# Attention with beacon keys, then an MLP: q and k turned by VectorE in 32x32 squares and placed through DRAM, one ring of four PSUM banks, seven MLP slots a step

One core of one Trainium2 chip. The metric is the device time of one execution in microseconds (us), median of several runs. The trace of a run shows one profiled execution, whose span is about 1.7 us shorter than its own time.

## The reference, cut to what matters

```python
B, H, S, Nb, D = (8, 8, 576, 16, 64)            # q, k, v: [B, H, S, D] f32; beacon_k, beacon_v: [B, H, Nb, D]
k_all = np.concatenate([beacon_k, k], axis=2)   # beacons are seen by every query, the rest is causal
scores = scale * np.matmul(q, k_all.transpose(0, 1, 3, 2))
scores = np.where(causal, -1000000000.0, scores)
a = softmax(scores)                             # written out in the reference
attn = np.matmul(a, v_all)
x = attn.transpose(0, 2, 1, 3).reshape(B * S, H * D)   # 4608 x 512
h = x @ w_in                                    # 512 -> 2048
g = h * (1.0 / (1.0 + np.exp(-1.702 * h)))
return g @ w_out                                # 2048 -> 512
```

The inputs of the attention are normal numbers times 0.1, so the scores are near zero and the softmax weights nearly equal. That matters for reading the experiments: **the comparison with the reference hardly sees q and k**.

## The kernel before

One step is one pair of heads of one batch: scores, exponentials, masks, and the product with v (AV) of the step before. Between these parts the loop deals out "slots" of the MLP, four matmuls of 512 columns each. The parts that the change touches:

```python
    psu = ctx.enter_context(tc.tile_pool(name="psu", bufs=3, space=bass.MemoryType.PSUM))
    pso = ctx.enter_context(tc.tile_pool(name="pso", bufs=1, space=bass.MemoryType.PSUM))
# ... (cut)
    def load_qk(b, h0, h1):
            # batches 1 to 7: one token a partition, 64 numbers (128 bytes in f16) a piece
            for i in range(NSB):
                rows = min(P, S - i * P)
                nc.gpsimd.dma_start(
                    out=t[0:rows, i, h0:h1, :],
                    in_=src[b, h0:h1, i * P : i * P + rows, :].rearrange("h s d -> s h d"),
                )
# ... (cut)
    def tr_pair(b, p, which):          # q (which 0) or k (which 1) of a pair of heads
            u = psu.tile([P, S], F16, tag="u", name="u")
            for i in range(NSB):       # five transposes on TensorE
                rows = min(P, S - i * P)
                nc.tensor.transpose(
                    u[:, i * P : i * P + rows],
                    src[0:rows, i, 2 * p : 2 * p + 2, :].rearrange("r h d -> r (h d)"),
                    ident[0:rows, 0:rows],
                )
        # then a copy to qT on ScalarE or to kT on VectorE
# ... (cut)
    def norm(b, hf):                   # four products by the reciprocals, all on GpSimd
# ... (cut)
    def mlp2(g, mt, qt):               # a second-layer tile in four slots, in the one bank of pso
        if qt == 0:
            ops[0] = pso.tile([P, DMODEL], F32, tag="o", name="o")
# ... (cut)
    QUOTA = 8                          # slots a step, spread evenly between the parts of a step
```

The normalising of a half batch is a chain of its own: the softmax sums are gathered to `zc`, VectorE takes the reciprocals `rc`, these go to DRAM (`zd`) and are read back spread over the partitions (`rz`), and four products write xT, from which the first layer reads.

The softmax here doesn't subtract the row's maximum and nothing guards it: scores larger than these inputs give would overflow.

## Time and profile before

| | before |
|---|---|
| median time | 477.54 us (476.39 to 480.32, 4 runs) |
| span of the profiled execution | 474.5 us |
| busy: TensorE, VectorE, ScalarE, GpSimd | 396, 193, 223, 251 us |
| mean granted TensorE clock | 0.941 |
| first MLP slot | 89.8 us |

I keep the division of the span that the prediction uses: the time to the first MLP slot, the TensorE work counted from there (341 us with transposes, 321 without), the end after the last matmul (about 4 us), and what is left, called **idle** below. For the kernel before it is 474.5 - 89.8 - 341 - 4 = 40 us.

### The profile page before, as it was taken

To read this page: it belongs to the slowest core of one execution; us is meant where nothing else is said; L and a number is where in the kernel's file an instruction comes from. 1 tells how busy PE (TensorE), PEld (TensorE's weight loads), DVE (VectorE), ACT (ScalarE), POOL (GpSimd) and SP (SyncE) were. 2 spreads that over 40 slices of the span, in tenths; PEclk is the share of its full clock that TensorE was granted. 3 is DMA by queue.
4 is the path that set the end of the run, shared out by engine and by line. 5 is a ranking of instruction groups with operands and counts; after the bars stand their busy time and mean duration, and the time that the engine had idled before them with its cause. 6 is when DMAs were issued, how large, how long until landed. Compare 5 with 4: busy or idle time off the path is not lost.

```text
span 474.5 us, 6853 instructions
## 1 busy us (share of the span) xinstructions
PE 396.0 (83%) x2584; PEld 201.8 (43%) x2584; DVE 193.0 (41%) x410; ACT 222.8 (47%) x341; POOL 251.3 (53%) x348
## 2 busy tenths in 40 slices
PE   2505555889999999899989998999899999899985
PEld 1303333444444444444444456645444444444432
DVE  5403373755125522561256226622561373184410
ACT  3303433665456545664466446644665442263421
POOL 9945078489528952895379627954616250400000
PEclk9955675899999999999999999999999999999999
DMA  9999939959614981399129911990203112100111
GB/s 86 157 176 179 82 46 148 79 44 111 111 59 56 111 122 46 65 107 129 47 55 110 134 48 52 108 140 34 63 2 95 56 42 64 77 1 22 46 44 66
DMA packets 122016, 38.22 MB, mean 81 GB/s; under 512 B 109696, under 2 KB 115328, under 8 KB 121984
## 3 DMA queue, kind: packets, MB, share of 16 engines
q0 software_dynamic: 111424, 18.62, 54.9%
q1 hardware_dynamic: 10560, 19.18, 14.2%
q8 instruction: 20, 0.33, 0.3%
q14 instruction: 12, 0.10, 0.1%
HBM read 46.66 MB, written 9.58 MB: 119 GB/s over the span
## 4 chain that ended last, share of the span: by engine, by line
PE 59%; ACT 17%; POOL 7%; DMA 7%; DVE 5%; issue 4%; ACTq 0%; POOLq 0%; DVEq 0%
PE o L408 26%; PE u L382 19%; ACT E L252 8%; PE u L310 6%; ACT sig L391 5%; PE u L189 4%; DVE g L392 4%; PE s L244 3%; ACT osb L417 3%; DMA w<-in_moe_w_in_dram 3%; DMA bk<-in_beacon_k_dram 2%; POOL kn L114 1%; POOL vb L136 1%; DMA zc<-O 1%; POOL xT L354 1%
## 5 line engine op out<-in xcount | busy, mean ns | idle before, releaser
L382 PE MATMUL u<-xT,w 128*128 128x512 f16 (+1 forms) x640 | 144.7, 358 | 12.5 <-DVE g L392 12.4
L408 PE MATMUL o<-w,g 128*128 128x512 f16 x576 | 144.1, 379 | 9.7 <-ACT osb L417 9.7
L392 DVE SCALAR_TENSOR_TENSOR g<-sig,u 128x512 f16<-128x512 f16 x144 | 99.0, 687 | 104.9 <-ACT sig L391 104.8
L354 POOL TENSOR_TENSOR xT<-O,rz 64x576 f16<-64x576 f32 x64 | 89.6, 1400 | 79.9 <-DMA rz<-zd 76.3
L391 ACT ACTIVATE sig<-u 128x512 f16<-128x512 f32 x144 | 87.6, 609 | 77.3 <-PE u L382 72.9
L252 ACT ACTIVATE E<-s 128x1024 f16<-128x1024 f32 (+3 forms) x128 | 104.7, 876 | 14.8 <-PE s L244 8.8
L317 DVE COPY O<-u 128x288 f32<-128x288 f32 x128 | 56.3, 453 | 71.2 <-PE u L310 69.9
L382 PEld LDWEIGHTS <-w 128*128 128x128 f16 x640 | 56.8, 97 | 63.3 <-issue 20.4
L274 POOL TENSOR_SCALAR_AFFINE_SELECT E<-E 128x256 f16<-128x256 f16 (+2 forms) x120 | 43.1, 395 | 67.0 <-ACT E L252 66.3
L408 PEld LDWEIGHTS <-g 128*128 128x128 f16 x576 | 50.2, 97 | 63.1 <-issue 15.6
L310 PE MATMUL u<-E,vb 128*128 128x288 f16 (+6 forms) x576 | 69.5, 260 | 5.3 <-DVE O L317 5.1
L310 PEld LDWEIGHTS <-vb 128*128 128x128 f16 (+1 forms) x576 | 52.5, 104 | 36.8 <-issue 12.2
L417 ACT ACTIVATE osb<-o 128x512 f32<-128x512 f32 x36 | 21.5, 597 | 82.1 <-PE o L408 82.1
L244 PE MATMUL s<-qT,kT 64*128 64x80 f16 (+5 forms) x384 | 44.1, 307 | 18.4 <-ACT E L252 9.9
L196 ACT COPY qT<-u 128x576 f16<-128x576 f16 x32 | 20.5, 640 | 73.4 <-PE u L189 66.7
L244 PEld LDWEIGHTS <-kT 64*128 64x128 f16 x384 | 17.1, 99 | 58.6 <-issue 46.2
L114 POOL DMA_DIRECT2D kn<-in_k_dram x35 | 29.6, 883 | 5.9 <-DMA w<-in_moe_w_in_dram 5.9
L136 POOL DMA_DIRECT2D vb<-in_v_dram x36 | 29.7, 860 | 2.7 <-DMA w<-in_moe_w_out_dram 2.7
L198 DVE COPY kT<-u 128x576 f16<-128x576 f16 x32 | 15.7, 492 | 37.2 <-PE u L189 35.6
L114 POOL DMA_DIRECT2D qn<-in_q_dram x35 | 29.9, 884 | 0.0
L168 PE MATMUL u<-ident,bk 16*128 16x16 f16 x32 | 2.1, 170 | 28.2 <-DMA bk<-in_beacon_k_dram 28.2
L267 DVE TENSOR_TENSOR E<-E,keep 128x128 f16<-128x128 f16 (+2 forms) x80 | 17.1, 271 | 14.0 <-ACT E L252 13.6
(29 smaller groups left out, 108.8 us busy)
## 6 DMA issues: line engine op xcount, KB each, us to landing
rz<-zd SPq DMA_DIRECT2D x32, 288.0 KB, 4.4
out_dram<-osb SPq DMA_DIRECT2D x36, 256.0 KB, 2.0
qn<-in_q_dram POOLq DMA_DIRECT2D x28, 128.0 KB, 4.2
kn<-in_k_dram POOLq DMA_DIRECT2D x28, 128.0 KB, 4.4
vb<-in_v_dram POOLq DMA_DIRECT2D x21, 128.0 KB, 6.0
w<-in_moe_w_in_dram POOLq DMA_DIRECT2D x4, 512.0 KB, 9.3
w<-in_moe_w_out_dram POOLq DMA_DIRECT2D x4, 512.0 KB, 9.5
vb<-in_v_dram POOLq DMA_DIRECT2D x7, 112.0 KB, 3.3
```

What stands on the lines that cost most here:

```text
L114: nc.gpsimd.dma_start(out=t[0:rows, i, h0:h1, :], in_=src[b, h0:h1, i * P : i * P + rows, :].rearrange("h s d -> s h d"),)
L244: nc.tensor.matmul(sc[:, x, o : o + e - a], kT[r : r + 64, p, j * P : (j + 1) * P], qT[r : r + 64, p, a:e], start=True, stop=True,)
L252: nc.scalar.activation(out=E[:, :, choff[ci] : choff[ci] + o], in_=sc[:, :, 0:o], func=AFT.Exp, scale=0.125,)
L274: nc.gpsimd.affine_select(out=blk, in_=blk, compare_op=ALU.is_ge, fill=0.0, base=mc, pattern=[[0, 2], [1, w]], channel_multiplier=-1,)
L310: nc.tensor.matmul(u[:, lo - qa : hi - qa], lhs, E[0:kw, x, col : col + hi - lo], start=(n == 0), stop=(n == len(mm) - 1),)
L317: nc.vector.tensor_copy(out=O[:, p % 2, qa:qe], in_=u[:, :])
L354: nc.gpsimd.tensor_tensor(out=xT[r : r + 64, p, c : c + S], in0=O[r : r + 64, a, :], in1=rz[r : r + 64, a, :], op=ALU.mult,)
L382: nc.tensor.matmul(u[:, o : o + w], w1t[:, kp, nt * P : (nt + 1) * P], xT[:, kp, m : m + w], start=(kp == 0), stop=(kp == NKP - 1),)
L391: nc.scalar.activation(out=sig[:, :], in_=u[:, :], func=AFT.Tanh, scale=0.851)
L392: nc.vector.scalar_tensor_tensor(out=gts[g][:, nt, :], in0=sig[:, :], scalar=1.0, in1=u[:, :], op0=ALU.add, op1=ALU.mult,)
L408: nc.tensor.matmul(o[:, :], gts[g][:, nt, mt * P : (mt + 1) * P], w2t[:, nt, :], start=(nt == 0), stop=(nt == NNT - 1),)
L417: nc.scalar.mul(out=osb[:, :], in_=o[:, :], mul=0.5)
```

## The change

Its intent is to take the transposes off TensorE, which bounds the steady stage, and to give TensorE enough PSUM banks. q and k are loaded so that a partition holds 18 consecutive tokens of a head (pieces of 4.6 KB of the input). VectorE turns them in squares of 32x32. The turned squares don't lie on the partitions where the scores want them, so they are stored to DRAM and read back in place. The products are split between VectorE and GpSimd, all matmuls but the scores share one ring of four banks, and a step gets seven slots in lumps. The diff, cut to its core (the order of loads at the start, forty warm-up matmuls and the loop's rewriting are cut):

```diff
-    psu = ctx.enter_context(tc.tile_pool(name="psu", bufs=3, space=bass.MemoryType.PSUM))
-    pso = ctx.enter_context(tc.tile_pool(name="pso", bufs=1, space=bass.MemoryType.PSUM))
+    psu = ctx.enter_context(tc.tile_pool(name="psu", bufs=4, space=bass.MemoryType.PSUM))
# ...
+    def load_qk(b, g, which):
+        nc.gpsimd.dma_start(
+            out=nat[b][which][:, g, :, :].rearrange("p t d -> p (t d)"),
+            in_=(q, k)[which][b, g * HG : (g + 1) * HG].rearrange("h (r t) d -> (h r) (t d)", t=TPP),
+        )
# ...
-    def tr_pair(b, p, which):
# ...
+    def tr_group(b, g, which):
# ...
+        dst = t[:, :, off : off + S].rearrange("p e (r t) -> p t e r", t=TPP)
+        n = TPP // 2
+        for c in range(2):
+            nc.vector.transpose(
+                dst[:, c * n : (c + 1) * n, :, :],
+                src[:, g, c * n : (c + 1) * n, :],
+            )
+        d = dr.tile([2, P, w], F16, tag=f"d{which}", name=f"d{which}")
+        for e in range(2):
+            nc.sync.dma_start(
+                out=d.rearrange("l (y e r) s -> e (l y) r s", y=2, e=2)[e],
+                in_=t[:, e, lo : lo + w],
+            )
+        full = (qTs, kTs)[which][b % 2]
+
+        def place():
+            nc.sync.dma_start(
+                out=full[:, 2 * g : 2 * g + 2, 0:w],
+                in_=d.rearrange("l p s -> p l s"),
+            )
# ...
+        (nc.vector, nc.gpsimd)[y].tensor_tensor(      # the products, in norm()
# ...
+    def mlp2(g, mt):
+        o = psu.tile([P, DMODEL], F32, tag="u", name="u")
+        for nt in range(NNT):
# ... in the loop, a step:
+        norm(b3, p3 // 2, 1); norm(b3, p3 // 2, 3)    # two lines in the source
+        mlp(4)
+        norm(b3, p3 // 2, 0); norm(b3, p3 // 2, 2)    # two lines in the source
# ... av, reciprocals
+        mlp(1)
# ... scores
+        while places:
+            places.pop(0)()
# ... av with mlp(1) between its halves
+            places += [tr_group(b + 1, p - 1, 1), tr_group(b + 1, p - 1, 0)]
+        mlp(1)
```

## The prediction

Its sum came to 414 us in the span, 65 + 321 + 24 + 4, and was taken down to 410 for the time. What rested on figures that no trace of this case shows is cut from the text, terms of the sum among them: how a turn of 576 elements came to 0.755 us and the small one to its price (both are in the 3.2 us of a half batch and in VectorE's 252), how long the new stores and their reading back take, and so the two steps between the transposes at 11 us and the scores near 18. For the turns the trace of before gives nearly the same: L392's 0.687 us for 512 elements, taken in proportion, is 0.77 for 576 and 3.2 for a half batch (an estimate). For the trip to DRAM it gives nothing, so that its "hidden" and the 7 us of it before the first scores had no measured ground. That the new stores run on four engines was expected too; the trace of the kernel after shows it, see `e4_stores16`.

> **What bounds the kernel now.** I read the slice view first, then busy time by windows, then the order of instructions in time, the waits and the groups by form.
>
> ```profile
> PE   2505555889999999899989998999899999899985
> DVE  5403373755125522561256226622561373184410
> POOL 9945078489528952895379627954616250400000
> PEclk9955675899999999999999999999999999999999
> DMA  9999939959614981399129911990203112100111
> ```
>
> A slice is 474.5 / 40 = 11.9 us. TensorE (PE) is half idle for eight slices, some 94 us, and nearly full afterwards; in the first five slices the DMA engines are full instead. So there are two stages with different limits. The windows give the sizes (columns: window, its length, busy time and count of PE, weight loads, DVE, ACT, POOL, then granted clock, DMA share, GB/s):
>
> ```profile
> 0.00:94.00 94.00, 46.02 (x397) 27.84 (x398) 39.50 (x123) 34.35 (x47) 60.30 (x82) 0.71 1.29 117
> ...
> 190.60:238.80 48.20, 44.54 (x292) 21.91 (x292) 19.92 (x39) 25.95 (x41) 32.23 (x47) 1.00 0.80 85
> ...
> 412.00:474.50 62.50, 55.68 (x256) 24.72 (x253) 22.02 (x32) 24.35 (x41) 0.00 (x0) 0.99 0.10 38
> ```
>
> The middle line is one steady batch (four steps, 32 MLP slots): PE 44.5 of 48.2 us busy at full clock, every other engine under 33. The last line is the tail, MLP alone. In both, TensorE is the bound. The start is a chain of loads and waits. These are the two places where TensorE stands first for data, then for buffers:
>
> ```profile
> PE u L168 <- DMA bk<-in_beacon_k_dram: 28.2, 3, 18.8
> ...
> PE u L382 <- DVE g L392: 12.4, 20, 0.7
> ...
> PE o L408 <- ACT osb L417: 9.7, 25, 0.7
> ```
>
> The beacon load is queued behind the weights and the second batch's q and k, so it stands for all of them. The other two are bank waits: first-layer matmuls (L382) for a bank of the ring of 3, second-layer ones (L408) for their only bank.
>
> What TensorE spends on each kind of work I take from starts in the order of time, since the durations overlap their successors:
>
> ```profile
> 195.50 0.52 PE L189 MATMUL u<-ident,qn 128*128 128x128 f16 x5
> 195.95 1.04 PE L382 MATMUL u<-xT,w 128*128 128x512 f16 x4
> ...
> 205.74 0.38 PE L310 MATMUL u<-E,vb 128*128 128x288 f16 x3
> 206.11 1.02 PE L382 MATMUL u<-xT,w 128*128 128x512 f16 x4
> 207.14 0.66 PE L310 MATMUL u<-E,vb 128*128 128x224 f16 x6
> 207.64 1.93 PE L382 MATMUL u<-xT,w 128*128 128x512 f16 x8
> ```
>
> Five transposes cost 195.95 - 195.50 = 0.45 us; the two AV halves of a head 0.37 and 0.50, so one step (two heads) 1.74. Read the same way at 198.25 to 201.38, the scores of one step cost about 1.04.
>
> ```profile
> 403.87 3.61 PE L408 MATMUL o<-w,g 128*128 128x512 f16 x16 [0.69 <-ACT osb L417]
> 408.17 3.61 PE L408 MATMUL o<-w,g 128*128 128x512 f16 x16 [0.69 <-ACT osb L417]
> 411.62 14.84 PE L382 MATMUL u<-xT,w 128*128 128x512 f16 x68
> ```
>
> Sixty-eight dense matmuls take 411.62 to 426.30, so 0.216 us each and 0.864 a slot of four. Two L408 tiles in a row lose 0.69 each to the single bank.
>
> [...] No run yet shows a transpose, [...]the 512-element DVE operation L392 takes 0.687 us[...]. [...](the 9 KB store of the reciprocals lands in 1.9 us, the 256 KB output in 2.0). [...] The new stores have a slowest dimension of 4 on the DRAM side[...]; no transfer of before shows such a case.
>
> **The change part by part.** *TensorE loses its transposes.* In the stage that it bounds (from the first MLP slot at 89.8 us) these are 42 groups of five (two of batch 2, 40 of batches 3 to 7): 42 x 0.45 = 19 us, and 1 us for the beacon. All of it lies on the path.
>
> *VectorE gains them.* Per half batch: four transposes of 576[...] and a small one[...] = 3.2 us, 16 times: 52 us. It gains 32 of the 64 normalising products (576 elements, 0.755: 24 us) and loses the kT copies (15.7 + 1.5). 193 + 52 + 24 - 17 = about 252 us, far from a bound overall. ACT loses 32 copies of 0.64 = 20.5 us. POOL loses 32 products of 1.40 (45 us) and swaps 78 q/k load issues, 65 us with L107, for 32. Beside TensorE, all this is off the path.
>
> *The DRAM trip.* A half batch is stored at the end of one step and read back in the middle of the next. [...] In steady state the data is wanted two steps after the store or later: hidden. For batch 0 it is on the path.
>
> *The start.* q and k of batch 0 are 1.18 MB in f16; the weights moved at 176 GB/s of f16 (third and fourth slice), so 1.7 us each for the four loads, with v in f32 beside them. First k and q on chip at about 7 and 9 us, transposes to 11[...]: **scores start near 18 us against 9.0 before**. In exchange the weights and batch 1 are queued together and q/k no longer come in rows of 128 bytes: from the gate at 18.5 us, w1 12 us, q/k of batch 1 7 us, so its first half can be turned by 36. VectorE waits there in order, after step 1. Then steps 2, 3, 4 and 5 at about 5 us (masks 2.7, O copies 1.8, turning 3.2 in some) bring 58; batch 2's q and k, issued behind a product that waits for its reciprocals, add about 5. **First MLP slot: about 65 us**, against 89.8. It also comes half a step earlier in the schedule (after step 6's scores, not step 7).
>
> *The ring of 4.* Second-layer tiles no longer have a single bank: most of the 9.7 us wait goes, and perhaps half of the 12.4.
>
> *Seven slots a step* move work from steps to the tail. TensorE's sum stays.
>
> **The sum.** From the first slot, TensorE still has 288 slots x 0.864 = 248.7; scores of 25 steps 26; AV of 26.5 steps 46: 321 us. Before, the same count plus 20 of transposes is 341, and from 89.8 to the last matmul's end at 470.5 there are 381, so 40 us of idle and small losses between groups. I take 9 off for the L408 bank, 6 for the ring, 3 for waits that the transposes themselves had, and add 2 for VectorE blocked by 3.2 us of turning: 24. The end after the last matmul stays 4 us. 65 + 321 + 24 + 4 = 414 in the span. The time lies 3 us above the span (477.5 against 474.5), but I trust the idle term least and think it too high, since the change was plainly scheduled to keep TensorE fed: I choose **410 us**, a ratio of 0.86.
>
> **The rivals.** (1) *VectorE becomes the bound.* A step with 7 first-layer slots has 7 x 0.69 + 4 x 0.45 + 3.2 + 1.5 = 11.3 us on VectorE against 9.0 on TensorE. For it: the trace already shows TensorE waiting for L392. Against: once the second layer runs, a step has about three such slots, so 8.6 at most and 6 in the mean. If a transpose costs twice my 0.755, some 14 of the 16 turns would each cost 1 to 3 us: 425 to 435. (2) *The start is not shortened.* The DRAM trip, the gate and VectorE's in-order waits add up to a first slot at 85 or later: then only the 20 of transposes and 18 of waits come off, about 435. For it: DMA is full in the first five slices and its bytes stay. Against: the 128-byte rows go. (3) *The transfers collide*: 19 MB more traffic delay the reciprocals (4.4 us to landing), on which the products, now on VectorE too, wait in order. Against: the rest of the DMA work shrinks. It would cost 0.5 us in each of 25 steps: 420. (4) *Everything fits as planned*: first slot at 58, idle 12: 395.
>
> **Range and chances.** The start is uncertain by 7 us, idle by 9; together about 11, so 8 in 10 between 395 and 426. Even rivals 1 and 2 stay over 8% faster. Chances: faster 0.97, same 0.02, slower 0.01.
>
> **What would show it.** Right: transposes of 0.7 to 0.8 us, VectorE near 250 us; no TensorE wait for the output copy; steps of 9 to 9.7 us, a steady batch near 38; first slot between 58 and 72 us, a dense tail of about 100 us. Wrong: TensorE waiting long for L383 (the former L392) or for qT and kT in steady steps; transposes over 1.2 us; a first slot after 80 us; a granted clock below 0.95 after it.

## More of the kernel before

Idle is a remainder and holds more than standing still: where matmuls take longer than the dense time that the 341 are worked out from, the excess is in it too. Here TensorE's busy time from the first slot on is 353.9 us, so 13 of the 40 us are of that kind.

## The result, and the profile after

**542.45 us** (540.69 to 545.91, 4 runs), against 477.54 of before: ratio **1.136** [1.128, 1.143]. The prediction was 410, and faster. Ratios here are the mean time of one kernel's fast runs over that of the other's fast runs of the same rounds, so they are not quite the ratio of the quoted medians.

In the slice view of the kernel after, a slice is 541.5 / 40 = 13.5 us:

```profile
PE   7041223435986789669865958596669999999997
DVE  5970891599749965995887489748874654426160
...
PEclk9565656557898788989977998799769999999999
```

TensorE is not full for two slices in a row before slice 31, near the end of the attention. VectorE, which had mostly twos and fives before, has eights and nines. The granted clock is below full speed in most slices in which TensorE has gaps; its mean is 0.839, where before had 0.941. The windows of the kernel after (start, four steady steps, tail; columns as in the prediction):

```profile
0.00:109.90 109.90, 39.40 (x227) 18.91 (x228) 66.15 (x114) 25.68 (x33) 23.34 (x39) 0.62 0.75 138
217.30:265.40 48.10, 38.05 (x238) 17.73 (x236) 38.57 (x48) 22.70 (x36) 21.98 (x36) 0.93 0.70 132
480.00:541.50 61.50, 57.70 (x268) 25.95 (x266) 22.01 (x32) 24.50 (x41) 0.00 (x0) 1.00 0.11 43
```

The four steps of the middle line have 238 matmuls where before had 292: the 40 transposes are gone, and 28 slots in place of 32 make 16 fewer. With so much less for TensorE to do they still take 48.1 us, and the steady batches, from first scores to first scores, take 51.1 to 53.5, where the prediction had "near 38". VectorE, at 38.6 us, is now as busy as TensorE; before it had 19.9. The tail is as it was. The first MLP slot comes at 109.9 us, against 65 predicted. Three rows of the costliest groups after (busy us, mean ns of one | idle before):

```profile
L170 DVE STREAM_TRANSPOSE tq<-qn 128x576 f16<-128x576 f16 x32 | 84.4, 2817 | 0.0
L170 DVE STREAM_TRANSPOSE tk<-kn 128x576 f16<-128x576 f16 x32 | 81.7, 2732 | 0.0
...
L156 DVE STREAM_TRANSPOSE tk<-bk 128x64 f16<-128x64 f16 x16 | 3.9, 245 | 18.5 <-DMA bk<-in_beacon_k_dram 18.4
```

A turn of 576 takes 2.8 us where 0.755 was predicted. The beacon's small turn, a ninth of the elements with writes that lie side by side, takes 0.245. That alone doesn't tell whether turns of 576 are slow as such or by their write step. Now the waits of the kernel after (engine, line, what it waited for: us in total, times, longest):

```profile
PE u L373 <- DVE g L383: 49.9, 8, 8.0
...
PE s L234 <- DMA qT<-d: 42.7, 3, 16.3
...
DVE xT L345 <- DMA rz<-zd: 26.8, 8, 9.3
```

The first is eight waits of 6.2 us in the mean, a different thing from the twenty short bank waits of before. In the order of time it looks so (start, us, engine, line, operation, [idle before]):

```profile
282.10 5.11 DVE L170 STREAM_TRANSPOSE tk<-kn 128x576 f16<-128x576 f16 x2
...
286.86 5.28 DVE L170 STREAM_TRANSPOSE tq<-qn 128x576 f16<-128x576 f16 x2
...
291.77 0.88 DVE L383 SCALAR_TENSOR_TENSOR g<-sig,u 128x512 f16<-128x512 f16 x1
```

```profile
292.70 1.87 PE L373 MATMUL u<-xT,w 128*128 128x512 f16 x4 [6.22 <-DVE g L383]
```

VectorE turns from 282.10 until the gating operation at 291.77 and empties no bank meanwhile; once it has run that one (L383), the first-layer matmuls go on after 6.22 us of idle. And at the start, the stores of the turned data on the chain that ended last, which the profile follows back from the last instruction, at each step to what released it (start, us, what):

```profile
20.95 5.29 DMA d<-tq
...
67.33 13.38 DMA d<-tq
...
84.35 7.29 DMA d<-tq
```

They were predicted to be on the path for batch 0 alone.

In terms of the prediction's sum, with 3.7 us for the end after the last matmul:

| term, us | predicted | after |
|---|---|---|
| first MLP slot | 65 | 109.9 |
| TensorE work from there | 321 | 321 |
| idle | 24 | 541.5 - 109.9 - 321 - 3.7 = 107 |
| end | 4 | 3.7 |

So 45 us are lost before the first slot and 83 after it. Of the 107 us of idle, 80 are waits of TensorE: the 49.9 above, 6.7 of the second layer for L383, 18.8 for the normalised xT and 5.0 for a bank that a copy of AV frees. Most of the rest is longer busy time, 346.7 us against 321, at a mean granted clock of 0.90 from the first slot on, where before had 1.00. That the clock lengthens it is not shown by a run of its own. The first theory: the **write step** of the turns makes VectorE slow and lumpy. The rivals: the **four-engine stores**, the order of transfers on the queue, the products on VectorE that wait for the reciprocals, seven slots in lumps, and traffic as such.

### The profile page after: what moved, and what is told of

The parts are those of the page before. It is cut to its first block, busy times and chain, and to the rows that moved or that the text cites. A ratio compares the mean times of both kernels' runs of the same rounds, so it can differ in the third digit from the quotient of the medians.

```text
span 541.5 us, 6200 instructions
## 1 busy us (share of the span) xinstructions
PE 386.1 (71%) x2216; PEld 185.9 (34%) x2216; DVE 353.0 (65%) x488; ACT 207.3 (38%) x314; POOL 153.4 (28%) x245
## 4 chain that ended last, share of the span: by engine, by line
PE 47%; DVE 31%; DMA 14%; issue 4%; ACT 2%; SPq 1%; POOL 0%; DVEq 0%; ACTq 0%
PE u L373 20%; PE u L395 18%; DVE tq L170 12%; DVE tk L170 12%; PE u L300 6%; DMA d<-tq 5%; DMA w<-in_moe_w_in_dram 3%; PE s L234 3%; DVE xT L345 2%; DVE g L383 2%; DVE O L307 2%; DMA rz<-zd 1%; DMA zc<-O 1%; DMA bk<-in_beacon_k_dram 1%; DMA bkf<-in_beacon_k_dram 1%
## 5 line engine op out<-in xcount | busy, mean ns | idle before, releaser
L373 PE MATMUL u<-xT,w 128*128 128x512 f16 (+1 forms) x640 | 156.5, 388 | 73.8 <-DVE g L383 49.9
L383 DVE SCALAR_TENSOR_TENSOR g<-sig,u 128x512 f16<-128x512 f16 x144 | 98.7, 697 | 86.2 <-ACT sig L382 85.9
L395 PE MATMUL u<-w,g 128*128 128x512 f16 x576 | 130.2, 381 | 6.7 <-DVE g L383 6.7
L300 PE MATMUL u<-E,vb 128*128 128x288 f16 (+6 forms) x576 | 76.1, 278 | 24.3 <-DVE O L307 20.0
L170 DVE STREAM_TRANSPOSE tq<-qn 128x576 f16<-128x576 f16 x32 | 84.4, 2817 | 0.0
L170 DVE STREAM_TRANSPOSE tk<-kn 128x576 f16<-128x576 f16 x32 | 81.7, 2732 | 0.0
L345 POOL TENSOR_TENSOR xT<-O,rz 64x576 f16<-64x576 f32 x32 | 45.8, 1449 | 93.1 <-DMA rz<-zd 91.9
L403 ACT ACTIVATE osb<-u 128x512 f32<-128x512 f32 x36 | 21.5, 598 | 93.2 <-PE u L395 93.2
L345 DVE TENSOR_TENSOR xT<-O,rz 64x576 f16<-64x576 f32 x32 | 26.6, 869 | 26.8 <-DMA rz<-zd 26.8
L133 POOL DMA_DIRECT2D vb<-in_v_dram x28 | 23.9, 865 | 1.1 <-DMA qn<-in_q_dram 0.6
L325 DVE RECIPROCAL rc<-zc 64x36 f32<-64x36 f32 x16 | 5.8, 361 | 11.2 <-DMA zc<-O 11.2
```

What stands on the lines that cost most here:

```text
L133: nc.gpsimd.dma_start(out=vb[0 : hi - lo, j, h0:h1, 0:D], in_=v[b, h0:h1, lo:hi, :].rearrange("h n d -> n h d"),)
L170: nc.vector.transpose(dst[:, c * n : (c + 1) * n, :, :], src[:, g, c * n : (c + 1) * n, :],)
L300: nc.tensor.matmul(u[:, lo - qa : hi - qa], lhs, E[0:kw, x, col : col + hi - lo], start=(n == 0), stop=(n == len(mm) - 1),)
L345: (nc.vector, nc.gpsimd)[y].tensor_tensor(out=xT[r : r + 64, 2 * hf + a, c : c + S], in0=(OA, OB)[y][r : r + 64, a, :], in1=rz[r : r + 64, ...
L373: nc.tensor.matmul(u[:, o : o + w], w1t[:, kp, nt * P : (nt + 1) * P], xT[:, kp, m : m + w], start=(kp == 0), stop=(kp == NKP - 1),)
L383: nc.vector.scalar_tensor_tensor(out=gts[g][:, nt, :], in0=sig[:, :], scalar=1.0, in1=u[:, :], op0=ALU.add, op1=ALU.mult,)
```

## The experiments

Eighteen kernels ran. Those with a ratio had three rounds against before on the same chip. They ran on five chips, on which before took 477.3 to 479.3 us, so between kernels that ran on different chips 2 us are no difference. No run tests the forty warm-up matmuls at the start, which came with the change.

### The write step of the turns

`e1_unit_stride` changes one line, so that a square's row is written side by side. The tokens then come out in another order. Its output is wrong, which doesn't matter for the time.

```diff
-        dst = t[:, :, off : off + S].rearrange("p e (r t) -> p t e r", t=TPP)
+        dst = t[:, :, off : off + S].rearrange("p e (t r) -> p t e r", t=TPP)
```

> The changed kernel, but each 32x32 turn writes its 32 elements side by side instead of 18 elements apart (tokens end up permuted, so the result is wrong on purpose; counts, sizes, loads and transfers are the same). Theory A, the write stride makes the turn slow: the 576-element turns fall from 2.8 us to about 0.75 us, VectorE's busy time from 353 to about 225 us, and the time to between 410 and 450 us. Rival B, a turn of this size is slow whatever it writes: turns stay at 2.7 to 2.8 us and the time at 542. Rival C, the DRAM trip and the start set the time: turns get fast, but the time stays over 500 us.

Measured: **502.86 us** (502.30 to 503.84), ratio 1.051 [1.048, 1.055]: 40 us less than the change. The group's row in this run:

```profile
L170 DVE STREAM_TRANSPOSE tk<-kn 128x576 f16<-128x576 f16 x32 | 22.3, 735 | 0.0
```

0.735 us: the prediction's 0.755 holds for writes that lie side by side. VectorE's total is 239.8 us, near the predicted 252. So the write step is shown, but 40 us of 132 is not the whole: the time stays over 500, as rival C wanted. The chain of this run names the next piece:

```profile
PE u L395 17%; PE u L373 17%; DMA d<-tq 13%; DMA rz<-zd 10%; DMA zd<-rc 7%; DMA zc<-O 5%; PE u L300 4%; DMA w<-in_moe_w_in_dram 3%; DVE xT L345 3%; DVE tk L170 2%; DVE tq L170 2%; PE s L234 2%; DVE O L307 2%; DVE g L383 1%; POOL xT L345 1%
```

13% of the span is a store of turned q. It stands six times on the chain, for 7.37 to 19.59 us.

`p1_probe` puts turns and copies of 576 elements, with different steps, behind the kernel before.

```diff
+    nc.vector.transpose(sc[:, 0 : 4 * N].rearrange("p (t r k) -> p t r k", r=32, k=4)[:, :, :, 0], s3)   # step 4
+    nc.vector.transpose(sc[:, 0:N].rearrange("p (r t) -> p t r", r=32), s3)                             # step 18
     # ... also steps 1, 2 and 8, and copies with a strided read or write on VectorE and ScalarE; three times each
```

> The kernel before, with turns and copies of 576 f16 elements added at its end, three of each form, for their durations alone. Theory A: a turn takes about 0.75 us with its 32 elements side by side, and about 2.8 us at 18 apart; the strides of 2, 4 and 8 elements show whether any step is slow or whether it grows with the step. Rival B: all turns take 2.8 us. The copies on VectorE and ScalarE, once reading at a stride and once writing at one, show whether the un-permuting could be done there: 0.75 us if a stride is free for a copy, 2.8 if it is not.

Measured, in the page's groups (lines 529, 531, 533, 535, 537: turns with write steps of 1, 2, 4, 8, 18 elements; 539 and 541: VectorE copies with a strided read, then a strided write; 543 and 545: the same on ScalarE):

```profile
L535 DVE STREAM_TRANSPOSE sc<-xT 128x576 f16<-128x576 f16 x3 | 8.2, 2736 | 0.1
L545 ACT COPY sc<-sc 128x576 f16<-128x576 f16 x3 | 8.0, 2651 | 0.1
L537 DVE STREAM_TRANSPOSE sc<-xT 128x576 f16<-128x576 f16 x3 | 7.9, 2640 | 0.1
...
L533 DVE STREAM_TRANSPOSE sc<-xT 128x576 f16<-128x576 f16 x3 | 4.4, 1460 | 0.1
L541 DVE COPY sc<-sc 128x576 f16<-128x576 f16 x3 | 4.2, 1399 | 0.1
L543 ACT COPY sc<-sc 128x576 f16<-128x576 f16 x3 | 3.5, 1155 | 17.2 <-DVE sc L541 17.2
...
L531 DVE STREAM_TRANSPOSE sc<-xT 128x576 f16<-128x576 f16 x3 | 2.5, 825 | 0.1
L529 DVE STREAM_TRANSPOSE sc<-xT 128x576 f16<-128x576 f16 x3 | 2.3, 779 | 0.1
...
L539 DVE COPY sc<-sc 128x576 f16<-128x576 f16 x3 | 1.9, 644 | 0.1
```

The turn costs 0.78, 0.83, 1.46, 2.74 and 2.64 us at steps of 1, 2, 4, 8 and 18: all of the loss is there at 8 elements (16 bytes), and a part at 4. VectorE's strided read, at 0.644 us, costs little (the probe has no dense copy; the kernel before's dense copy of 576 elements from PSUM to kT takes 0.492); its strided write costs twice that. A dense turn and a copy with a strided read, 0.78 + 0.64 us, are thus cheaper than a turn with a strided write, 2.64. The run took 505.98 us with its tail of tests; that is one run, and no comparison.

`e2_token_rows` makes e1 right by construction: each partition takes tokens r, 32 + r, 64 + r and so on of its head, in pieces of 128 bytes of f16, and the dense write then puts token s at column s.

```diff
-        nc.gpsimd.dma_start(
-            out=nat[b][which][:, g, :, :].rearrange("p t d -> p (t d)"),
-            in_=(q, k)[which][b, g * HG : (g + 1) * HG].rearrange("h (r t) d -> (h r) (t d)", t=TPP),
-        )
+        for x in range(HG):
+            nc.gpsimd.dma_start(
+                out=nat[b][which][x * SQ : (x + 1) * SQ, g, :, :],
+                in_=(q, k)[which][b, g * HG + x].rearrange("(t r) d -> r t d", r=SQ),
+            )
```

> As the run before it, but with q and k loaded so that the result is right: row r of a head holds tokens 32t + r, in pieces of 64 elements (128 bytes once cast), four issues for each half instead of one. Theory A expects turns of 0.75 us and right results. If the larger loads of 18 tokens were worth much, this is slower than the run with unit stride by the extra DMA work at the start, 10 to 20 us; if DMA is hidden, within 2 per cent of it.

Measured: 512.36 us, ratio 1.071 [1.066, 1.075]. Short pieces cost 9.5 us over e1, while the stores still bound.

### The stores on four engines

`e4_stores16` keeps the slow turns and cuts the two stores into four, each with a slowest dimension of 32 on both sides.

```diff
-        for e in range(2):
+        for x in range(HG):
             nc.sync.dma_start(
-                out=d.rearrange("l (y e r) s -> e (l y) r s", y=2, e=2)[e],
-                in_=t[:, e, lo : lo + w],
+                out=d.rearrange("l (y e r) s -> (l y) r e s", y=2, e=2)[x],
+                in_=t[x * SQ : (x + 1) * SQ, :, lo : lo + w],
             )
```

> The changed kernel with its slow turns, but each store to DRAM goes out as four transfers of 32 rows each, whose slowest dimension is 32, instead of two whose slowest dimension on the DRAM side is 4. If the stores are slow because they use four DMA engines, the waits behind stores of tq (13.4 and 7.3 us on the chain of waits) shrink to some 3 us each, scores start 3 us earlier, and the time falls by 15 to 30 us. If they are slow because they stand behind the bulk loads on every engine, the time stays within 1 per cent of 542.

Measured: 528.33 us, ratio 1.106 [1.101, 1.112], 14 us less than the change. The number of engines can be counted. The packets line of the kernel after:

```profile
DMA packets 76382, 57.94 MB, mean 107 GB/s; under 512 B 45120, under 2 KB 65600, under 8 KB 76352
```

And of e4:

```profile
DMA packets 78175, 57.96 MB, mean 110 GB/s; under 512 B 46912, under 2 KB 67392, under 8 KB 78144
```

The data rows are the same. The trace of the kernel after has stretches in which one kind of transfer moves alone. From 376.0 to 379.8 us it is a pair of k stores: the DMA share of that window is 0.26 of 16 engines, **about four**, at 78 GB/s. From 529.0 to 529.5 us it is an output store: the share is 1.00, at 389 GB/s. Its packet records show that the pair comes with 8 packets of four bytes, so 4 a store, and the output store with 16. Counted like that, 64 stores on 4 engines have 256 of these packets, and 128 stores on 16 would have 2048: 1792 more. The class under 512 bytes grew by exactly 1792: e4's stores come with 16 each, like the output store.

`e5_unit_16` has both edits (and e1's wrong order of tokens).

> Unit-stride turns (first experiment, result still wrong on purpose) and stores as four transfers of 32 rows. The unit-stride run left 503 us, 90 over the prediction, and its chain of waits stands at the stores (12 per cent) and at the three small transfers of the reciprocals, which share the in-order SyncE queue with them (zc 6.3, zd 6.9 us a time, against 2.3 and 1.9 before). If four-engine stores are the cause, both shrink and the time falls below 485. If the sharing of the queue is the cause whatever the engines, it falls by less than 14 us, which is what the same edit gave with slow turns.

Measured: **446.33 us** (444.3 to 447.19), ratio 0.933 [0.928, 0.939]. One edit gave 40, the other 14, **both together 96 us**. The two causes hide one another. My reading of it: while the turns are slow, TensorE stands for them anyway and a late store costs little (5% of the chain after); when they are fast, the store is what the rest waits for (13% in e1). The chain of e5:

```profile
PE u L373 20%; PE u L395 20%; DMA rz<-zd 11%; DMA zd<-rc 6%; PE u L300 5%; DMA qn<-in_q_dram 3%; DVE xT L345 3%; DMA d<-tq 3%; PE s L234 3%; DMA zc<-O 3%; SPq L176 2%; DVE g L383 2%; POOL xT L345 2%; DMA bkf<-in_beacon_k_dram 2%; DVE O L307 1%
```

The store fell from 13% to 3%. The reciprocals' trip (zc, zd, rz) now holds 20%; in the same line of the kernel before, zc with 1% is all that is listed of it. The first slot is at 86.2 us and the idle is 35.

### What is left: queue order, the start, bytes, products

`e6_late_place` is e5 with the reading back moved behind the gathering of the sums, so that it no longer stands ahead of the reciprocals' spread on the same queue. In the kernel after, SyncE's queue stands 58.1 us in all for stores of turned q before it issues the reading back (15 waits, the longest 10.3).

```diff
-        while places:
-            places.pop(0)()
         if i >= 2 and p2 % 2 == 1 and b2 < B:
             z_spread(b2, p2 // 2)
# ... av
                 z_gather(b1, p1 // 2)
+        while places:
+            places.pop(0)()
```

> As the run before it, and the reading back is issued at the end of the step, behind the gather of the sums, instead of ahead of the spreading of the reciprocals, so that no transfer of the reciprocals stands behind a wait for a store. If that wait in the queue is what delays the products (rz, zd and zc on the chain), the time falls by another 10 to 25 us and VectorE's and GpSimd's waits for rz shrink to less than half; if the transfers themselves are slow, nothing changes by more than 1 per cent.

Measured: 453.20 us in the three fast runs (a fourth was slow), ratio 0.947 [0.940, 0.955], about 7 us slower than e5, a miss. VectorE's wait for the reciprocals doesn't shrink, but goes from 37.8 to 45.3 us. The queue's order is not the cause.

`e8_start_order` is e6 with q and k of batch 1 and the beacons of batches 1 to 7 loaded ahead of the first layer's weights.

```diff
-    for c in range(4):
-        load_w1(c)
     for f in batch_loads(1):
         f()
     load_bk(1, B)
+    for c in range(4):
+        load_w1(c)
```

> As the run before it, and behind the gate q, k and the beacons of batches 1 to 7 are loaded ahead of the first weights instead of behind them. The first turn of batch 1 stood 17 us for the beacons, which stood for the weights. If the start is that chain, the turn comes at about 35 instead of 51 us, the first MLP matmul 10 to 15 us earlier and the time falls by as much; if the start is then held by the stores or the weights, it falls by less than 4 us.

Measured: 447.30 us, ratio 0.937 [0.929, 0.945], first slot at 78.7 us instead of e6's 84.2. Against e6 it gains some 6 us, where 10 to 15 were hoped for.

`e14_small_trip` is e5 with only 64 of the 576 or 592 columns stored and read back (q and k wrong, the rest zeroed): the same transfers with a ninth of the bytes.

```diff
-                in_=t[x * SQ : (x + 1) * SQ, :, lo : lo + w],
+                in_=t[x * SQ : (x + 1) * SQ, :, lo : lo + 64],
# ... the DRAM side and the reading back likewise
```

> Unit-stride turns and 16-engine stores, but only 64 of the 576 or 592 columns go to DRAM and back (wrong on purpose; the rest of qT and kT is set to zero once). Same number of transfers and of waits, a ninth of the bytes. If the bytes of the trip are what delays the start and the reciprocals (rz, zd, zc), the time falls from 446 to 415 to 430 and VectorE's wait for rz below half of its 38 us. If the waits in the queue and the schedule are the cause, it stays within 1 per cent of 446.

Measured: 432.41 us, ratio 0.904 [0.900, 0.909], 14 us under e5. The first slot comes at 79.1, and VectorE's wait for the reciprocals falls from 37.8 to 28.9 us. So the bytes of the trip are worth 14 us, about half in the start; the wait did not halve, as it should have if they delayed the reciprocals. That is no gain to be had: the bytes are the trip.

`e9_late_products` is e5 with the four products moved behind the last scores of the step, so that VectorE doesn't stand for the reciprocals.

```diff
-        if i >= 3 and p3 % 2 == 1 and b3 < B:
-            norm(b3, p3 // 2, 1)
-            norm(b3, p3 // 2, 3)
# ... the other two likewise
         pool(3)
+        if i >= 3 and p3 % 2 == 1 and b3 < B:
+            for n in (1, 3, 0, 2):
+                norm(b3, p3 // 2, n)
```

> Unit-stride turns and 16-engine stores (446 us), and the four normalising products moved half a step later, behind the third and fourth score chunk, so that the spread reciprocals have a whole step to arrive. If VectorE's in-order wait for rz (38 us in all there) is what still keeps TensorE idle, that wait falls below 10 us and the time to 425 to 437. If TensorE's idle time is at the start and elsewhere, the time stays within 1 per cent of 446, or rises since the MLP starts half a step later.

Measured: 466.09 us, ratio 0.974 [0.969, 0.978], a miss: 20 us slower than e5, although VectorE's wait for the reciprocals fell from 37.8 to 11.2 us. In the order of time:

```profile
228.02 0.58 PE L373 MATMUL u<-xT,w 128*128 128x512 f16 x1 [5.28 <-POOL xT L345]
```

The batch is released to the first layer right behind these products, so TensorE now waits for them: 37.3 us on those of GpSimd, 13.8 in e5.

`e11_hybrid` is e9 with e8's order at the start and with q and k right by construction: batches 0 and 1 keep the long loads, are turned densely into a buffer and permuted by a copy with a strided read; the others use e2's rows.

```diff
+        if b < 2:
+            m = tp.tile([P, TPP, 2, SQ], F16, tag="tm", name="tm")
+            dst = m[:, :, :, :]
# ... the two turns as in e1
+        if b < 2:
+            for e in range(2):
+                nc.vector.tensor_copy(
+                    out=t[:, e, off : off + S].rearrange("p (r t) -> p r t", t=TPP),
+                    in_=m[:, :, e, :].rearrange("p t r -> p r t"),
+                )
```

> A right version of all that: late products, 16-engine stores, loads of batch 1 ahead of the weights, and turns at unit stride: batches 0 and 1 from the loads of 18 tokens with a VectorE copy that reads at a stride (0.64 us for 576 elements in the probe), batches 2 to 7 from token rows. Within 2 per cent of the run with late products if the token rows and the copies are hidden; some 10 us slower if the token rows cost in steady state what they cost in the first pair of runs (9.5 us).

Measured: 467.25 us, ratio 0.977 [0.971, 0.982], as e9. `e17_mended` puts the products back to where the change has them. It is **the change with its two faults mended**, right by construction, and with the better order at the start.

> The change mended, with right results: unit-stride turns (18-token loads and a strided VectorE copy for batches 0 and 1, token rows from batch 2), 16-engine stores, q, k and beacons of batch 1 ahead of the weights, products where the change has them. If the other start order helps by the 7 to 9 us by which the first MLP matmul came earlier in its run, and token rows are hidden: 436 to 448 us. If token rows cost in steady state too: 450 to 458.

Measured: **445.89 us** (444.05 to 447.02), ratio 0.931 [0.927, 0.935]; first slot 79.7, idle 38. That is the time of e5, though the first slot comes 6.5 us earlier: what the order of loads gained at the start is lost after it. The short rows are a candidate. GpSimd issues 96 loads of them in 63 us, and e5's 24 long ones for the same batches would take some 14 (an estimate from its 0.58 us each). No run parts this.

Is the rest a schedule that is half a step too tight? `e18_late_both` takes e11 (late products) and releases a batch half a step later as well; `e19_late_ready` takes e17 and delays the release alone.

```diff
-        if i >= 3 and p3 == 3 and b3 < B:
+        if i >= 3 and p3 == 3 and b3 == 0:
             ready[0] = b3
# ... at the start of the next step
+        if i >= 4 and p3 == 0:
+            ready[0] = max(ready[0], min(b3 - 1, B - 1))
```

> The mended change with the four products moved after the third and fourth score chunks (as in e9) and with the batch released to the first layer one half step later still, at the start of the next step (batch 0 is released as before). Theory A: what the mended change still loses (38 us of idle TensorE) is a schedule that is half a step too tight; early products block VectorE on the reciprocals, late products make the first layer wait, so only moving both helps: 430 to 436 us, TensorE's wait for xT under 6 us instead of 18.9, VectorE's wait for rz near 11. Theory B: the idle comes from elsewhere (lumps of sixteen matmuls, the transfers of the trip, the start): 444 to 452 us, near the 446 of the mended change, although both waits fall. The late products alone cost 20 us (467 against 447).

> The mended change with the batch released to the first layer half a step later, the products where the change has them. Theory A: TensorE's wait for xT (18.9 us) goes but VectorE still waits 42 us for the reciprocals in order: 436 to 442 us. Theory B: 444 to 450 us.

Measured: e18 **443.82 us** (442.25 to 445.72), ratio 0.927 [0.921, 0.933]; e19 449.94 (447.88 to 454.21), 0.941 [0.933, 0.950]. In e18 VectorE's wait for the reciprocals is 9.2 us (42.2 in e17), and this transfer is gone from the chain's large shares. Late products together with a late release undo the 20 us of e9's miss, as theory A wanted, but against e17 (on another chip) the time moves by 2 us where it wanted 10 to 16. Removing VectorE's largest wait leaves the time where it was.

This doesn't clear late products, though. What counts is what TensorE itself waits for, and there theory A's condition, under 6 us for xT, wasn't met: after the first slot TensorE waits 18.9 us for products in e17, and in e18 still 17.2 (9.6 for those of GpSimd, 7.6 for those of VectorE). On e18's chain GpSimd holds 15% of the span, 6% of it issuing the short rows of q and k. With them out of the way the products might come earlier; that was not tried.

### The ring, and seven slots

`e7_ring4_before` is the **kernel before** with the PSUM part of the change alone. That is two edits at once: four shared banks, and second-layer tiles whole, 16 matmuls in one lump and not four lumps of four. TensorE's transposes and eight slots are kept.

```diff
-    psu = ctx.enter_context(tc.tile_pool(name="psu", bufs=3, space=bass.MemoryType.PSUM))
-    pso = ctx.enter_context(tc.tile_pool(name="pso", bufs=1, space=bass.MemoryType.PSUM))
+    psu = ctx.enter_context(tc.tile_pool(name="psu", bufs=4, space=bass.MemoryType.PSUM))
# ... mlp2: all 16 matmuls in the first of its four slots, into a tile of psu; the other three empty
```

> The kernel before with only the PSUM part of the change: second-layer tiles whole (16 matmuls together) and in one ring of 4 banks. The prediction took 9 us off for the output copy's bank and 6 for the ring. If that holds, 460 to 470 us (ratio 0.97 to 0.98) and no TensorE wait for the output copy; if the lumps of 16 matmuls delay the attention work as much as the bank gave, within 1 per cent of 477.5.

Measured: **440.89 us** (438.61 to 443.3), ratio 0.923 [0.916, 0.930]. The steady batch in the windows:

```profile
158.30:201.35 43.05, 42.53 (x293) 21.52 (x294) 19.60 (x39) 25.94 (x41) 31.95 (x46) 1.00 0.86 95
```

43.05 us, of which TensorE is busy 42.53, for a batch that took 48.2. Its first slot comes at 93.9 (it was 89.8), and the idle is 441.6 - 93.9 - 341 - 3.7 = 3 us. The prediction gave the ring 15.

Where did 37 us of idle go? From the first slot on, TensorE's waits for banks that the ring now shares fall from 22.1 us (12.4 and 9.7) to 2.2, and its whole time without work from 30.8 to 7.9. The other 14 us are busy time, 353.9 to 339.8, and they lie in the second layer. Its rows before, here, and in e10, the next run, which has whole tiles but the single bank:

```profile
L408 PE MATMUL o<-w,g 128*128 128x512 f16 x576 | 144.1, 379 | 9.7 <-ACT osb L417 9.7
...
L407 PE MATMUL u<-w,g 128*128 128x512 f16 x576 | 129.3, 379 | 0.0
...
L396 PE MATMUL o<-w,g 128*128 128x512 f16 x576 | 131.2, 380 | 12.8 <-DVE g L384 6.7
```

With whole tiles this busy time is near 130 us whether the ring is there or not. So of e7's 36 us I put some 22 down to the banks and 14 to the whole tiles. That is a division read from the traces; no run of the kernel before has one edit without the other.

`e10_no_ring` is the change without the ring (three banks and one); its second-layer tiles stay whole.

```diff
-        o = psu.tile([P, DMODEL], F32, tag="u", name="u")
+        o = pso.tile([P, DMODEL], F32, tag="o", name="o")
```

> The changed kernel with the PSUM banks as before: a ring of 3, and one bank of its own for second-layer tiles (still 16 matmuls together). In the kernel before the ring alone gave 36 us. If it gives as much inside the change, this is 570 to 580 us; if TensorE there waits for VectorE and transfers anyway, so that banks hardly matter outside the tail, 545 to 560.

Measured: 565.31 us, ratio 1.182 [1.177, 1.187]. Inside the change the ring by itself gives 23 us, near the 22 read above and less than the 36 of e7 with its whole tiles.

`e12_quota7_before` sets QUOTA from 8 to 7 in the kernel before, nothing else.

> The kernel before with 7 MLP slots a step instead of 8, nothing else. TensorE's sum stays, work moves to the tail; in the tail the single bank costs 0.69 us for each tile that follows another. The prediction counted this part as nothing: within 2 per cent of 477.5. If the slots matter by themselves, because fewer bank waits fall into the steps or more into the tail, more than that.

Measured: 462.21 us, ratio 0.967 [0.962, 0.972]: 15 us less. The waits for the banks that the ring of before had, 12.4 and 9.7 us, are 4.2 and 3.5 here, so 14 us less.

`e15_ring_start` is e7 with q, k and beacons of batch 1 ahead of the weights, and each batch's loads issued ahead of the products in GpSimd's order:

```diff
+    new_nat(1)
+    new_qk(1)
+    load_qk(1, 0, H)
+    load_bk(1)
     load_w1(0)
# ... in the loop: new_nat, load_qk, load_bk and load_v moved ahead of run_later(i)
```

> The kernel before with the PSUM part (441 us), TensorE's transposes kept, and another load order only: q and k of batch 1 ahead of the first weights, and each later batch's loads ahead of the products of the same step, which wait for their reciprocals. TensorE is busy 42.5 of 43.05 us in its steady batches, so only the start is left: if the first MLP matmul then comes at 70 to 80 us instead of 93, the time is 418 to 430 us; if the start is bound by the bytes and not by their order, it stays within 1 per cent of 441.

Measured: **433.69 us** (432.92 to 434.27), ratio **0.906** [0.903, 0.909], the fastest kernel that computes the right thing, though short of the 418 to 430 expected: first slot 83.7 where 70 to 80 was hoped for, idle 4. `e16_ring_start_q7` sets its QUOTA to 7.

> As the run before it, with 7 MLP slots a step. In the kernel before alone 7 slots gave 15 us, which I put down to fewer bank waits. If that is so, nothing is left to give here: within 1 per cent of the run with 8. If 7 slots help by themselves, 10 us less.

Measured: 451.79 us in the three fast runs (449.52 to 452.59; a fourth was slow), ratio 0.943 [0.938, 0.947], 18 us slower than e15, which neither theory expected. Seven slots helped the kernel short of banks and hurt the one that has them. After the first slot TensorE waits 12.9 us here for the banks of the scores, against 1.0 in e15; the rest of the 18 us isn't explained.

## Why the prediction was wrong, point by point

**The turns: the step that failed.** The prediction's 0.755 us for a turn of 576 holds for dense writes (0.735 in e1). The change writes 36 bytes apart, and a turn took 2.8 us. The write step was in the diff, and I priced the elements only. The trace of before holds no turn by VectorE, so nothing in it could show what a write step costs; the probe does, 0.78 us at a step of 1 and 2.64 at 18. Rival 1 had the mechanism and its sign, "if a transpose costs twice my 0.755", but sized it at 425 to 435: the turns came at 3.7 times, and the blocks of VectorE at 10 us each. I had given every block 1 to 3 us.

**The stores: seen, and wrongly called hidden.** That they would run on four engines was right, as the DMA share of 0.26 and the count of 1792 show. "Hidden" was wrong. A pair of k stores that moves alone takes about 4 us (in the change, the window above); a store of q that held up the chain for 13.38 us there did so while the DMA share was 0.70 of 16 engines, so beside other transfers. In e1 the six on the chain take 7.37 to 19.59 us. The same data on 16 engines lands in 3.5 and 2.6 us at the median (e5), and the pieces on e5's chain, half as large, take 1.67 to 6.93. Why a store on four engines takes so long beside others is not shown. That 16 engines, in twice as many and half as large transfers, are worth 14 us with slow turns and 57 with fast ones (503 to 446) is measured.

**The first slot, 65.** It came at 109.9. Dense turns bring it to 104.1, 16 engines alone to 95.6, both to 86.2, and the order of loads to 79.7 in e17. Rival 2 ("a first slot at 85 or later") was right in kind. The last 15 us between 79.7 and 65 are not settled; the trip's bytes are 7 of them by e14 (79.1 against e5's 86.2).

**The idle, 24.** It is 107 in the change, 38 in the mended one. "9 for the L408 bank, 6 for the ring" was too little: the banks are worth some 22 us in the kernel before, all of what the waits view showed, and 23 inside the change (e10). What I took for "small losses between groups" was in good part the second layer in lumps of four: whole tiles take 14 us off TensorE's busy time (e7), and I gave them nothing. So this term was mis-sized in the change's favour, and the turns and stores swamped it. The sum itself said 414 for the span, 417 for the time; taking it down to 410 was a guess that the idle would be smaller still, and it went the wrong way.

**The products.** Rival 3 ("the transfers collide", 10 us) is partly borne out: e14's bytes are 14 us. That VectorE stands for the reciprocals is true (37.8 us in e5), but e9 and e18 show that this wait can be moved without any gain, as long as TensorE goes on waiting for the products.

**Seven slots.** That they "move work from steps to the tail" priced them at nothing. In the kernel before they are worth 15 us, with the ring, whole tiles and e15's order of loads they cost 18. Whether they help or harm the mended change was not tried.

**What held.** No transposes on TensorE, and no wait of it for the output copy; VectorE's total once the turns are dense (239.8 in e1 against 252); the end. The list of signs at the prediction's end was good: turns over 1.2 us (2.8), a first slot after 80 (109.9), long waits for L383 (49.9 us in eight) and a granted clock below 0.95 (0.90) all came.

**Where the change stands.** The kernel before with the PSUM part gives 441, the change with both faults mended 446 (444 in e18): with intervals that overlap, no better. The fairer pair is e15 and e17, which both load batch 1 ahead of the weights and ran in the same rounds: 433.7 against 445.9, so the kernel that keeps its transposes on TensorE is 12 us faster, if with eight slots and its products all on GpSimd. e17's first slot comes 4 us earlier than e15's, but from there it takes 362.6 us against 348.9, with 20 us less to do. So the 20 us that leave TensorE are more than lost again in what came with the move.

The trace of e17 shows in part where. Of its 38 us of idle, TensorE waits 18.9 for products and 8.9 for banks that VectorE's copies of AV free, and some 9 are busy time: 329.4 us, where e7's 339.8 less 20 of transposes leave 320, at a mean clock of 0.96 against e7's 1.00. Why the products and copies are late stays **open**. It isn't the queue's order (e6), nor VectorE's wait for the reciprocals alone (e18); the trip's bytes explain about 8 us (35 to 26.5, e14); lumps of sixteen matmuls alone can't be it, since e7 has them and idles 3. The short rows' issues on GpSimd and the seven slots are candidates. Seven slots raise the idle from 4 (e15) to 23 us (e16) where the transposes stay on TensorE; but what TensorE waits for there after the first slot, the scores' banks (12.9 us), it hardly waits for in the mended change (0.6), and no run parts them.

## What to carry to other kernels

Price an operation by its access pattern and not by its count of elements: move a stride from the write to the read (a turn with the strided write took 2.64 us, a dense turn and a copy with a strided read 0.78 + 0.64), and count the engines that a store uses (about 4 of 16 here, all 16 once it was cut by rows of the tile), then test the two edits together, since each hid the other (40 and 14 us alone, 96 together). Short waits for a PSUM bank, "0.7 us longest", add up (45 of them to 22 us), and a tile of 16 matmuls dealt out in fours cost another 14 us as busy time, which no list of waits shows; so try one more bank in the ring and whole tiles before rebuilding anything. Ask what the bounding engine itself waits for: removing 33 us of VectorE's wait in e18 moved the time by 2 us. Try each part of a bundle by itself: here one part, the PSUM banks with whole tiles, was worth as much as all of it after mending.
